# Two recurrent attention layers on one core: softmax denominators through a ones matrix and Ln/Exp, a mask cut like the scores, projections chunk by chunk, and filler matmuls spread over all segments

## The chip, the cores and the metric

The kernel runs as one program on one core of a Trainium2 chip. The metric is the device time of one execution in microseconds (us), of which the median of three runs is given. All times of the trace come from one further execution, recorded by the hardware profiler.

## The reference

Two kinds of layer alternate, A and B, twice each, every one with a layer norm ahead of it and a residual around it. The change lies in A. A walks over 2048 tokens in 64 segments of 32. Each segment sees the 32 tokens and 8 memory rows, and the memory rows of the next segment are the first 8 rows of this one's output, so the segments depend on each other one after the other.

```python
def _A_ref(x, mem0, Wq, Wk, Wv, Wo, seg_len):     # 32 heads of 128, Dm = 512, M = 8, seg_len = 32
    mask = (idx[:, None] < M) | (idx[:, None] >= idx[None, :])
    mem = mem0
    for s in range(n_seg):                         # 64
        xs = x[:, s * seg_len:(s + 1) * seg_len, :].copy()
        h = jnp.concatenate([mem, xs], axis=1)     # 40 rows
        q = jnp.einsum('btd,dhe->bhte', h, Wq)     # k and v likewise, from Wk and Wv
        scores = jnp.einsum('bhqe,bhke->bhqk', q, k) * scale
        scores = jnp.where(mask[None, None], scores, -1000000000.0)
        p = _softmax(scores, axis=-1)
        o = jnp.einsum('bhqk,bhke->bhqe', p, v)
        o = jnp.einsum('bhte,hed->btd', o, Wo)
        mem = o[:, :M, :].copy()
        outs.append(o[:, M:, :])
    return jnp.concatenate(outs, axis=1)

x = x + _A_ref(_layernorm(x), A_mem0, A_Wq, A_Wk, A_Wv, A_Wo, A_seg_len)
x = x + _B_ref(_layernorm(x), B_w_in, B_w_sp, B_b_sp, B_w_out)   # gelu, a 2048 x 2048 mixing, two projections
# and both once more
```

## The kernel before

Four stages follow one another: A, B, A, B (`a_block` and `b_block`). In an A stage the order of the instructions on TensorE, VectorE (DVE), ScalarE (ACT) is the order of the code; SyncE and GpSimd, which issue the transfers and some small copies, are ordered by the scheduler.

**Rows of a segment.** The 40 rows of a segment are split in two. `hA` holds, transposed, the 8 memory rows and the first 24 tokens, 32 columns; it is ready only when the segment before has given its memory rows. `hBs` holds the last 8 tokens, which depend on nothing; `hB` has those of four segments together (a block `tb` of 128 tokens, 16 blocks; `j4` is the segment's number within its block).

**One segment, in the order of TensorE's work** (`segment`, from L546; the names are those of its tiles):

- `psm`: Q and K of the `hA` rows, four chunks of 512 columns, 16 matmuls of 128x32 each. Four of these matmuls (one `kt`) lie side by side in the four column groups of the array. `mm_pair` (L409) builds two chunks at once; the second of the pair uses `_mm_held` (L39 to 45), which is why half of these matmuls stand under L42. ACT copies each chunk to `rows` (L565), DVE transposes it into `QQ` or `KK` (L571).
- `psv`: V of all 40 rows, four chunks again, built in pairs; ACT copies chunks 0 and 2 to `vs`, DVE chunks 1 and 3 (L583).
- For each half of the heads: a mask matmul into `psS` over 320 columns (L587, `maskN` holds -30000), 16 small score matmuls on top of it (L591), `E` = exp on ACT (L594), four matmuls of `E` with the indicator `ind` which give the denominators of 8 heads as a column `psD` (L599), a reciprocal on DVE into `Rc`, eight matmuls that spread `Rc` over the rows again (`probs`, L608), and the product `PT` on DVE (L612). These steps stand between pieces of V.
- `psO`: 16 matmuls of `vs` with `PT` (`pv`, L621). Its columns go to `uT` of this segment (8 memory rows, L624), to `uT` of the next (24 token rows, L628) and to `oB` (8 rows, DVE, L629).
- `pw`: the output projection of `uT`, 128 matmuls of 128 columns (`wo_pass`, L493), one half behind each `psO`. The second `psO` has the same two PSUM banks as the first (pool `attO`), so it begins when all three copies of the first are done.
- `build_hA` (L535 to 539): DVE puts the memory rows from `pw` into `pre` and transposes that into the next `hA`, on which the next segment's `psm` waits.

**Fillers.** Work that belongs to other segments stands behind the second `psO` and behind `pw`, in two equal parts. `j4` = 0: `y_pass`, the projection of the last block's `oB` (`pwB`, 128 matmuls, 64 in each place). `j4` = 1 and 2: `bpass`, Q and K of the next block's `hB` (`psb`, 32 matmuls of 512 columns, 16 in each place). `j4` = 3: nothing. Beside that a block has `ln_load`, `ln_apply`, `ln_turn` (the next block's normed rows by DVE and transfers), `y_load` and `y_stats` (residual and statistics of the last block).

**PSUM.** Eight banks: four of pool `acc` (`psm`, `psv`, `psb`, `pw`, `pwB` in turn), two of `att` (`psS`, `psD`), two of `attO` (`psO`).

The lines that call the fillers:

```python
            ov1 = pv(1)
            for f in fillers:
                next(f)
            for _ in wo_pass(pw, uT_cur, 1):
                pass
            if s + 1 < NSEG:
                build_hA(s + 1, pw)
            for f in fillers:
                next(f, None)
```

## Time and profile before

| | |
|---|---|
| median of 3 runs | 2440.13 us (2438.45 to 2441.03) |
| the profiled execution's own time | 2444.6 us |
| its span, first to last instruction | 2442.7 us |
| TensorE matmul (PE) busy | 2093.6 us, 86%, 52992 instructions |
| TensorE weight load (PEld) busy | 1242.0 us, 51%, 52992 instructions |
| VectorE (DVE) busy | 1130.0 us, 46% |
| ScalarE (ACT) busy | 879.5 us, 36% |
| GpSimd (POOL) busy | 241.3 us, 10% |
| mean granted TensorE clock | 0.97 of full speed |

A matmul's own duration does not say what it costs TensorE: four matmuls of 512 columns that lie side by side in the array are each 0.39 us long and overlap. So the time of a piece of work is read from the starts of consecutive groups in the timeline, and idle time from the bracket at a row's end, which names how long the engine stood before it and what released it. "issue" there means that the engine waited for nothing that the profile shows. The two A stages take about 1900 us of the span.

### The profile page before, as it was taken

To read this page: it belongs to the slowest core of one execution; us is meant where nothing else is said; L and a number is where in the kernel's file an instruction comes from. 1 tells how busy PE (TensorE), PEld (TensorE's weight loads), DVE (VectorE), ACT (ScalarE), POOL (GpSimd) and SP (SyncE) were. 2 spreads that over 40 slices of the span, in tenths; PEclk is the share of its full clock that TensorE was granted. 3 is DMA by queue.
4 is the path that set the end of the run, shared out by engine and by line. 5 is a ranking of instruction groups with operands and counts; after the bars stand their busy time and mean duration, and the time that the engine had idled before them with its cause. 6 is when DMAs were issued, how large, how long until landed. Compare 5 with 4: busy or idle time off the path is not lost.

```text
span 2442.7 us, 114595 instructions
## 1 busy us (share of the span) xinstructions
PE 2093.6 (86%) x52992; PEld 1242.0 (51%) x52992; DVE 1130.0 (46%) x2489; ACT 879.5 (36%) x1956; POOL 241.3 (10%) x567
## 2 busy tenths in 40 slices
PE   0799999999999999872968999999999999997799
PEld 0355555555555555441754555555555555554466
DVE  2454455554555555440434555555554555553422
ACT  0343344443434344360003434444434444343700
POOL 1100000000000000001220000000000000000022
PEclk9999999999999999985989999999999999999899
DMA  9111111111111110128550111111111111102253
GB/s 361 49 31 31 31 31 32 33 31 31 31 31 31 31 32 27 65 80 249 146 171 20 32 31 31 31 31 31 31 32 32 37 31 31 29 22 82 74 125 104
DMA packets 178719, 145.98 MB, mean 60 GB/s; under 512 B 97472, under 2 KB 148288, under 8 KB 175168
## 3 DMA queue, kind: packets, MB, share of 16 engines
q1 hardware_dynamic: 152544, 83.76, 12.7%
q10 hardware_dynamic: 21728, 30.78, 3.6%
q0 software_dynamic: 3968, 24.12, 2.7%
q8 instruction: 415, 6.80, 1.2%
q14 instruction: 64, 0.52, 0.1%
HBM read 88.13 MB, written 33.70 MB: 50 GB/s over the span
## 4 chain that ended last, share of the span: by engine, by line
PE 75%; ACT 9%; DMA 6%; issue 5%; DVE 4%; POOL 1%; SPq 0%; ACTq 0%; POOLq 0%; DVEq 0%
PE psv L416 12%; PE psm L42 10%; PE psm L416 9%; PE psv L42 8%; PE pg L222 7%; PE pw L493 5%; PE psO L621 4%; PE psS L591 3%; ACT vs L583 3%; PE psD L608 3%; PE pwB L493 3%; PE psD L599 3%; DMA wspT<-in_B_w_sp_dram 2%; PE psb L416 2%; PE psS L587 2%
## 5 line engine op out<-in xcount | busy, mean ns | idle before, releaser
L416 PE MATMUL psm<-Wq_sb,hA 128*32 128x512 bf16 x4096 | 420.8, 386 | 35.1 <-DVE hA L539 31.2
L42 PE MATMUL psm<-Wk_sb,hA 128*32 128x512 bf16 x4096 | 420.1, 385 | 15.7 <-ACT rowsB L481 11.6
L416 PE MATMUL psv<-Wv_sb,hA 128*32 128x512 bf16 x2048 | 406.5, 385 | 0.0
L416 PE MATMUL psv<-Wv_sb,hBs 128*32 128x512 bf16 x2048 | 405.3, 385 | 0.0
L42 PE MATMUL psv<-Wv_sb,hA 128*32 128x512 bf16 x2048 | 400.0, 379 | 0.0
L42 PE MATMUL psv<-Wv_sb,hBs 128*32 128x512 bf16 x2048 | 398.7, 379 | 0.0
L565 ACT CAST rows<-psm 128x512 bf16<-128x512 f32 x512 | 275.0, 589 | 254.9 <-PE psm L416 253.5
L416 PEld LDWEIGHTS <-hA 128*32 128x32 bf16 x6144 | 232.3, 96 | 214.2 <-DVE hA L539 60.2
L42 PEld LDWEIGHTS <-hA 128*32 128x32 bf16 x6144 | 241.0, 97 | 164.9 <-issue 41.5
L493 PE MATMUL pw<-Wo_sb,uT 128*32 128x128 bf16 x16640 | 284.5, 219 | 33.6 <-issue 19.9
L493 PEld LDWEIGHTS <-uT 128*32 128x32 bf16 x16640 | 256.1, 97 | 83.5 <-issue 24.8
L571 DVE STREAM_TRANSPOSE QQ<-rows 128x512 bf16<-128x512 bf16 x256 | 181.3, 708 | 167.6 <-ACT rows L565 167.6
L612 DVE TENSOR_TENSOR PT<-E,psD 128x320 bf16<-128x320 bf16 x256 | 125.0, 488 | 237.0 <-PE psD L608 144.8
L222 PE MATMUL pg<-wspT,z2n 128*128 128x256 bf16 (+1 forms) x1536 | 177.0, 277 | 56.8 <-DMA wspT<-in_B_w_sp_dram 56.8
L624 ACT CAST uT<-psO 128x128 bf16<-128x128 f32 x256 | 68.0, 266 | 362.1 <-PE psO L621 362.1
L222 PEld LDWEIGHTS <-z2n 128*128 128x128 bf16 (+1 forms) x1536 | 151.4, 100 | 82.2 <-issue 64.3
L416 PE MATMUL psb<-Wq_sb,hB 128*32 128x512 bf16 x1024 | 104.1, 393 | 98.2 <-DVE hB L464 74.3
L538 DVE CAST_PREDICATED pre<-maskM,pw 128x128 bf16<-128x128 uint16 x126 | 36.7, 291 | 317.0 <-PE pw L493 317.0
L583 ACT CAST vs<-psv 128x512 bf16<-128x512 f32 x256 | 149.9, 585 | 77.0 <-PE psv L416 77.0
L583 DVE CAST vs<-psv 128x512 bf16<-128x512 f32 x256 | 176.1, 688 | 0.0
L571 DVE STREAM_TRANSPOSE KK<-rows 128x512 bf16<-128x512 bf16 x256 | 171.4, 670 | 0.3 <-ACT rows L565 0.3
L594 ACT ACTIVATE E<-psS 128x320 bf16<-128x320 f32 x256 | 111.9, 437 | 120.2 <-PE psS L591 120.2
(98 smaller groups left out, 2550.9 us busy)
## 6 DMA issues: line engine op xcount, KB each, us to landing
xs<-xd SPq DMA_DIRECT2D x48, 256.0 KB
xs<-xd ACTq DMA_DIRECT2D x48, 256.0 KB
oA_d<-o_sb SPq DMA_DIRECT2D x130, 64.0 KB
xs_y<-xd SPq DMA_DIRECT2D x32, 256.0 KB
xd<-ot_y SPq DMA_DIRECT2D x32, 256.0 KB
Wq_sb<-in_A_Wq_dram POOLq DMA_DIRECT2D x6, 1024.0 KB, 17.5
Wk_sb<-in_A_Wk_dram POOLq DMA_DIRECT2D x6, 1024.0 KB, 25.8
Wv_sb<-in_A_Wv_dram POOLq DMA_DIRECT2D x6, 1024.0 KB, 20.6
```

What stands on the lines that cost most here:

```text
L42: return te.add_instruction(mybir.InstMatmult(name=nc.get_next_instruction_name(), engine=mybir.EngineType.PE, start_tensor_calc=start, st ...
L222: nc.tensor.matmul(pg[0:fsz, :], lhsT=z2n[:, st_i, f0:f0 + fsz], rhs=wspT[:, st_i, :], start=(st_i == 0), stop=(st_i == NT - 1))
L416: nc.tensor.matmul(o, lhsT=lhs(cg), rhs=rhs2[i](kt, cg), start=st, stop=sp_, tile_position=(0, 32 * cg))
L493: nc.tensor.matmul(po[32 * cg:32 * cg + 32, 0:128], lhsT=lhs[:, h, :], rhs=wo_rhs(h, cg), start=(n == 0), stop=(n == H - 1), tile_position ...
L565: nc.scalar.copy(r[:], ps2[i][:])
L571: nc.vector.transpose(out=(QQ, KK)[i][:, half, :, 0:32], in_=rows[i][:])
L583: (nc.vector.tensor_copy if i else nc.scalar.copy)(vs[:, 4 * c:4 * c + 4, :].rearrange("p h e -> p (h e)"), ps2[i][:])
L591: nc.tensor.matmul(psS[64 * g:64 * g + 40, hl, :], lhsT=KK[:, half, 8 * g + hl, :], rhs=QQ[:, half, 8 * g + hl, :], start=False, stop=True ...
L594: nc.scalar.activation(out=E[half][:], in_=psS[:], func=ACT.Exp, scale=scale)
L599: nc.tensor.matmul(psD[half][0:80, 2 * w:2 * w + 2], lhsT=E[half][:, 2 * w:2 * w + 2, :].rearrange("p h q -> p (h q)"), rhs=ind[:, 0:2], s ...
L612: nc.vector.tensor_tensor(out=PT[half][:], in0=E[half][:], in1=psD[half][:, 128:448].rearrange("p (h q) -> p h q", q=40), op=ALU.mult)
L621: nc.tensor.matmul(psO[:, g, 40 * hl:40 * hl + 40], lhsT=vs[64 * g:64 * g + 40, 8 * half + hl, :], rhs=PT[half][64 * g:64 * g + 40, hl, :] ...
```

## The change

Numbers of lines below are those of the changed kernel where they differ.

- **Denominators.** One matmul of the block matrix `ones64` (two blocks of 64 x 64 ones) with `E` puts the sum over the keys into every row of `psD`, 320 columns. ACT takes Ln of it into `L` and exp(-L) into `R`; `PT` = `E` x `R` on DVE. The four matmuls with `ind`, the reciprocal and the eight spreading matmuls go. One instruction loads ACT's function table with exp and ln ahead of each A stage.
- **Mask.** Two matmuls, of 64 columns of weights each, in the tiling of the scores, in place of one.
- **Chunks.** Q, K and V are built chunk by chunk (`mm_chunk`), Q and K in the order 0, 2, 1, 3; ACT copies V chunks 0, 1 and 2, DVE chunk 3.
- **Fillers.** Each segment now has 32 matmuls of `pwB` behind the second `psO` (`fill_a`) and one chunk of `psb`, 16 matmuls, behind `pw` (`fill_b`). `pwB` keeps its bank through all four segments. The output loads and statistics of a block come a block later, the next block's rows are loaded earlier, and `prep_segment` stands at the segment's end.

```diff
+        def mm_chunk(ps, lhs, rhs, kts=range(KT)):
+            for kt in kts:
                 for cg in range(4):
...
+                    nc.tensor.matmul(ps[32 * cg:32 * cg + 32, :], lhsT=lhs(kt, cg), rhs=rhs(kt, cg),
+                                     start=(kt == 0), stop=(kt == KT - 1), tile_position=(0, 32 * cg))
...
+        nc.scalar.add_instruction(mybir.InstLoadActFuncSet(name=nc.get_next_instruction_name(), engine=mybir.EngineType.Activation,
+                                                           act_func_set_id=LN_EXP_SET, ins=[], outs=[]))
...
         def bpass(tb, j):
...
+            ps = acc.tile([P, 512], F32, name="psb")
+            mm_chunk(ps, lambda kt, cg: bs["hB"][:, kt, :], lambda kt, cg: qk_rhs(j, kt, cg))
+            r = rowp.tile([P, 512], BF16, name="rowsB", bufs=2)
+            nc.scalar.copy(r[:], ps[:])
...
         def y_pass(tb):
             pwB = acc.tile([P, DM], F32, name="pwB")
-            for n, _ in enumerate(wo_pass(pwB, blk_state[tb]["oB"])):
-                if n == 1:
-                    yield
+            for _ in wo_pass(pwB, blk_state[tb]["oB"]):
+                yield
...
-                (nc.vector.tensor_copy if i else nc.scalar.copy)(vs[:, 4 * c:4 * c + 4, :].rearrange("p h e -> p (h e)"), ps2[i][:])
+                (nc.vector.tensor_copy if c == 3 else nc.scalar.copy)(vs[:, 4 * c:4 * c + 4, :].rearrange("p h e -> p (h e)"), ps[:])
...
-                nc.tensor.matmul(psS[:], lhsT=ident_bf[:], rhs=maskN[:].unsqueeze(1).to_broadcast([P, 8, 40]),
-                                 start=True, stop=True, skip_group_check=True)
+                for g in range(2):
+                    nc.tensor.matmul(psS[64 * g:64 * g + 64], lhsT=ident_bf[:, 64 * g:64 * g + 64],
+                                     rhs=maskN[:].unsqueeze(1).to_broadcast([P, 8, 40]),
+                                     start=True, stop=True, tile_position=(0, 64 * g), skip_group_check=True)
...
             def denom(half):
-                psD[half] = att.tile([P, 512], F32, name="psD")
-                for w in range(4):
-                    nc.tensor.matmul(psD[half][0:80, 2 * w:2 * w + 2], lhsT=E[half][:, 2 * w:2 * w + 2, :].rearrange("p h q -> p (h q)"),
-                                     rhs=ind[:, 0:2], start=True, stop=True)
...
+                psD = att.tile([P, 8, 40], F32, name="psD")
+                nc.tensor.matmul(psD[:], lhsT=ones64[:], rhs=E[half][:], start=True, stop=True)
+                L = segp.tile([P, 8, 40], F32, name="L")
+                nc.scalar.activation(out=L[:], in_=psD[:], func=ACT.Ln)
+                R[half] = segp.tile([P, 8, 40], BF16, name="R")
+                nc.scalar.activation(out=R[half][:], in_=L[:], func=ACT.Exp, scale=-1.0)
...
             def probs(half):
-                for w in range(4):
-                    for g in range(2):
-                        nc.tensor.matmul(psD[half][64 * g:64 * g + 64, 128 + 80 * w:208 + 80 * w],
-                                         lhsT=Rc[half][0:80, 2 * w + g:2 * w + g + 1].to_broadcast([80, 64]), rhs=ident_bf[0:80, 0:80],
-                                         start=True, stop=True, tile_position=(0, 64 * g))
                 PT[half] = segp.tile([P, 8, 40], BF16, name="PT")
-                nc.vector.tensor_tensor(out=PT[half][:], in0=E[half][:], in1=psD[half][:, 128:448].rearrange("p (h q) -> p h q", q=40), op=ALU.mult)
+                nc.vector.tensor_tensor(out=PT[half][:], in0=E[half][:], in1=R[half][:], op=ALU.mult)
...
             scores(0)
-            v_kt(0, v0, 2)
-            v_kt(0, v0, 3)
-            v_out(0, v0, 0)
+            qk_T(3, r3)
+            v_mm(0, range(2, 4), v0)
             denom(0)
+            v_out(0, v0)
+            v1 = v_mm(1, range(0, 2))
             scores(1)
...
+            def fill_a():
+                next(yp, None)
+
+            def fill_b():
+                if tb + 1 < NB:
+                    bpass(tb + 1, (0, 2, 1, 3)[j4])
+                if j4 == 3:
+                    next(yp, None)
...
-        y_load(NB - 1)
-        y_stats(NB - 1)
+        for tb in (NB - 2, NB - 1):
+            y_load(tb)
+            y_stats(tb)
```

What stands in a row on the engines afterwards, at three places:

ACT, one segment before, from the last copies of Q and K to the copies of the second `psO` (`E` is the exp, `vs` the copies of V, `uT` those of `psO`):

```order
L565 CAST rows<-psm 128x512 x4
L594 ACTIVATE E<-psS 128x320
L583 CAST vs<-psv 128x512
L594 ACTIVATE E<-psS 128x320
L624 CAST uT_316<-psO 128x2x8x8
L583 CAST vs<-psv 128x512
L628 CAST uT_315<-psO 128x2x8x24
L624 CAST uT_316<-psO 128x2x8x8
L543 COPY o_sb<-pw 128x128
L628 CAST uT_315<-psO 128x2x8x24
```

and the same stretch of the changed kernel:

```order
L538 CAST rows<-psm 128x512 x4
L565 ACTIVATE E<-psS 128x320
L571 ACTIVATE L<-psD 128x320
L573 ACTIVATE R<-L 128x320
L552 CAST vs<-psv 128x512
L565 ACTIVATE E<-psS 128x320
L571 ACTIVATE L<-psD 128x320
L573 ACTIVATE R<-L 128x320
L552 CAST vs<-psv 128x512 x2
L589 CAST uT_308<-psO 128x2x8x8
L593 CAST uT_307<-psO 128x2x8x24
L589 CAST uT_308<-psO 128x2x8x8
```

Each exp has two more passes behind it, the first copy of V stands behind those of half 0 and ahead of the exp of half 1, and both other copies of V stand ahead of the first copy of `psO`.

TensorE around the first denominators, before (each matmul has its weight load ahead of it; `ident_bf` and `maskN` are the mask's):

```order
L42 LDWEIGHTS hBs_301
L42 MATMUL psv<-Wv_sb,hBs_301 32x512
L599 LDWEIGHTS E
L599 MATMUL psD<-ind,E 80x2
L599 LDWEIGHTS E
L599 MATMUL psD<-ind,E 80x2
L599 LDWEIGHTS E
L599 MATMUL psD<-ind,E 80x2
L599 LDWEIGHTS E
L599 MATMUL psD<-ind,E 80x2
L587 LDWEIGHTS ident_bf
L587 MATMUL psS<-maskN,ident_bf 128x320
```

and now:

```order
L399 LDWEIGHTS hBs_293
L399 MATMUL psv<-Wv_sb,hBs_293 32x512
L569 LDWEIGHTS ones_83
L569 MATMUL psD<-E,ones_83 128x320
L399 LDWEIGHTS hA_291
L399 MATMUL psv<-Wv_sb,hA_291 32x512
```

One matmul stands for four, and a piece of V stands between it and the second mask.

TensorE at the end of a segment that had no filler (`j4` = 3), the last matmul of `pw` and the next segment's first `psm`, before:

```order
L493 LDWEIGHTS uT_32285
L493 MATMUL pw<-Wo_sb,uT_32285 32x128
L416 LDWEIGHTS hA_32270
L416 MATMUL psm<-Wq_sb,hA_32270 32x512
```

and now, with the row of `psb` standing for 16 of its kind:

```order
L471 LDWEIGHTS uT_31254
L471 MATMUL pw<-Wo_sb,uT_31254 32x128
L399 LDWEIGHTS hB
L399 MATMUL psb<-Wq_sb,hB 32x512
...
L399 LDWEIGHTS hA_31239
L399 MATMUL psm<-Wq_sb,hA_31239 32x512
```

A chunk of `psb` stands between the two in every segment.

## Rows read from the trace of the kernel before

**Rows 1.** The page: one transfer queue, and the chain by engine.

```profile
q8 instruction: 415, 6.80, 1.2%
...
PE 75%; ACT 9%; DMA 6%; issue 5%; DVE 4%; POOL 1%; SPq 0%; ACTq 0%; POOLq 0%; DVEq 0%
```

**Rows 2.** Waits of TensorE by releaser: us in total, times, longest.

```profile
PE psO L621 <- DVE oB L629: 48.8, 128, 0.5
...
PE pwB L493 <- issue: 29.5, 19, 4.0
...
PE pw L493 <- issue: 19.9, 23, 3.9
```

**Rows 3.** Timeline, TensorE, two segments' starts: start, length, instruction [idle before, releaser].

```profile
82.56 0.61 PE L416 MATMUL psm<-Wq_sb,hA 128*32 128x512 bf16 x4 [2.21 <-DVE hA L539]
...
1017.97 0.62 PE L416 MATMUL psm<-Wq_sb,hA 128*32 128x512 bf16 x4 [0.74 <-DVE hA L539]
```

**Rows 4.** Timeline, TensorE, one segment of the first attention stage, the middle.

```profile
502.54 0.31 PE L587 MATMUL psS<-maskN,ident_bf 128*128 128x320 bf16 x1
502.78 0.38 PE L591 MATMUL psS<-QQ,KK 128*40 128x40 bf16 x16
503.09 0.39 PE L416 MATMUL psv<-Wv_sb,hA 128*32 128x512 bf16 x1
...
504.07 0.31 PE L599 MATMUL psD<-ind,E 128*80 128x2 bf16 x4
...
504.77 0.39 PE L416 MATMUL psv<-Wv_sb,hA 128*32 128x512 bf16 x1
...
505.32 0.33 PE L608 MATMUL psD<-ident_bf,Rc 80*64 80x80 bf16 x8
505.58 0.39 PE L416 MATMUL psv<-Wv_sb,hA 128*32 128x512 bf16 x1
```

**Rows 5.** Timeline, the same segment: ACT, DVE and the second psO.

```profile
503.26 0.44 ACT L594 ACTIVATE E<-psS 128x320 bf16<-128x320 f32 x1 [0.55 <-PE psS L591]
...
507.93 0.59 ACT L583 CAST vs<-psv 128x512 bf16<-128x512 f32 x1 [0.34 <-PE psv L416]
...
508.15 0.69 DVE L583 CAST vs<-psv 128x512 bf16<-128x512 f32 x1
...
508.42 0.48 ACT L628 CAST uT<-psO 128x384 bf16<-128x384 f32 x1
...
508.93 0.29 DVE L629 CAST oB<-psO 128x128 bf16<-128x128 f32 x1
...
509.37 0.37 PE L621 MATMUL psO<-PT,vs 40*128 40x40 bf16 x16 [0.38 <-DVE oB L629]
...
509.67 1.08 PE L493 MATMUL pwB<-Wo_sb,oB 128*32 128x128 bf16 x64
```

**Rows 6.** Timeline, TensorE, the end of a segment without filler.

```profile
437.28 1.08 PE L493 MATMUL pw<-Wo_sb,uT 128*32 128x128 bf16 x64 [0.35 <-ACT uT L624]
439.11 0.40 PE L416 MATMUL psm<-Wq_sb,hA 128*32 128x512 bf16 x4 [0.75 <-DVE hA L539]
```

**Rows 7.** Timeline, TensorE, two places with issue ahead of a row.

```profile
155.16 0.79 PE L493 MATMUL pw<-Wo_sb,uT 128*32 128x128 bf16 x42 [0.70 <-issue]
...
569.94 0.62 PE L493 MATMUL pwB<-Wo_sb,oB 128*32 128x128 bf16 x30 [0.26 <-issue]
570.35 1.11 PE L493 MATMUL pw<-Wo_sb,uT 128*32 128x128 bf16 x64
571.24 0.67 PE L493 MATMUL pwB<-Wo_sb,oB 128*32 128x128 bf16 x34
...
573.96 0.92 PE L493 MATMUL pwB<-Wo_sb,oB 128*32 128x128 bf16 x30 [2.05 <-issue]
```

**Rows 8.** Timeline, the first attention stage's last transfers: ACT and DVE.

```profile
1042.76 0.27 ACT L504 COPY oB_sb<-pwB 128x128 f32<-128x128 f32 x1 [6.90 <-PE pwB L493]
...
1048.95 0.69 DVE L112 BATCH_NORM_STATS2 bnst<-ot_y 128x6 f32<-128x512 f32 x1 [15.28 <-POOL ot_y L517]
```

More of the change, by code (lines that the diff above doesn't have):

```diff
@@ L544, in store_o, with segment @@
             nc.sync.dma_start(oA_d[s], o_sb[:])
-        def segment(s, fillers):
+        def segment(s, fill_a, fill_b):
             tb, j4 = s // 4, s % 4
@@ L554, in segment @@
             oB = blk_state[tb]["oB"]
-            E, PT, psD, Rc = [None] * 2, [None] * 2, [None] * 2, [None] * 2
-            def qk(half):
-                ps2 = [acc.tile([P, 512], F32, name="psm") for _ in range(2)]
-                for kt in range(KT):
-                    mm_pair(ps2, lambda cg: hA_cur[:, kt, :],
-                            [lambda kt, cg, jj=jj: qk_rhs(jj, kt, cg) for jj in (half, half + 2)], kt)
-                rows = []
-                for i in range(2):
-                    r = rowp.tile([P, 512], BF16, name="rows", tag="rowsQK", bufs=4)
-                    nc.scalar.copy(r[:], ps2[i][:])
-                    rows.append(r)
-                return rows
@@ L569, in qk_T @@
-            def qk_T(half, rows):
-                for i in range(2):
-                    nc.vector.transpose(out=(QQ, KK)[i][:, half, :, 0:32], in_=rows[i][:])
-            def v_start():
-                return [acc.tile([P, 512], F32, name="psv") for _ in range(2)]
-            def v_kt(half, ps2, kt):
-                def rhs(c):
-                    return lambda kt, cg: Wv_sb[:, kt, 2048 * (cg // 2) + 512 * c:2048 * (cg // 2) + 512 * c + 512]
-                mm_pair(ps2, lambda cg: (hA_cur if cg % 2 == 0 else hB_cur)[:, kt, :], [rhs(2 * half), rhs(2 * half + 1)], kt)
@@ L581, in v_out, with qk @@
-            def v_out(half, ps2, i):
-                c = 2 * half + i
-                (nc.vector.tensor_copy if i else nc.scalar.copy)(vs[:, 4 * c:4 * c + 4, :].rearrange("p h e -> p (h e)"), ps2[i][:])
+            E, PT, R = [None] * 2, [None] * 2, [None] * 2
+            def qk(j):
+                ps = acc.tile([P, 512], F32, name="psm")
+                mm_chunk(ps, lambda kt, cg: hA_cur[:, kt, :], lambda kt, cg: qk_rhs(j, kt, cg))
+                r = rowp.tile([P, 512], BF16, name="rows", tag="rowsQK", bufs=4)
+                nc.scalar.copy(r[:], ps[:])
+                return r
@@ new lines, in qk_T, with v_mm, v_out @@
+            def qk_T(j, r):
+                nc.vector.transpose(out=(QQ, KK)[j // 2][:, j % 2, :, 0:32], in_=r[:])
+            def v_mm(c, kts, ps=None):
+                if ps is None:
+                    ps = acc.tile([P, 512], F32, name="psv")
+                mm_chunk(ps, lambda kt, cg: (hA_cur if cg % 2 == 0 else hB_cur)[:, kt, :],
+                         lambda kt, cg: Wv_sb[:, kt, 2048 * (cg // 2) + 512 * c:2048 * (cg // 2) + 512 * c + 512], kts)
+                return ps
+            def v_out(c, ps):
+                (nc.vector.tensor_copy if c == 3 else nc.scalar.copy)(vs[:, 4 * c:4 * c + 4, :].rearrange("p h e -> p (h e)"), ps[:])
@@ L585, in scores @@
             def scores(half):
                 psS = att.tile([P, 8, 40], F32, name="psS")
[L587 to L588 removed]
+                for g in range(2):
+                    nc.tensor.matmul(psS[64 * g:64 * g + 64], lhsT=ident_bf[:, 64 * g:64 * g + 64],
+                                     rhs=maskN[:].unsqueeze(1).to_broadcast([P, 8, 40]),
+                                     start=True, stop=True, tile_position=(0, 64 * g), skip_group_check=True)
@@ L662, in segment @@
             ov1 = pv(1)
-            for f in fillers:
-                next(f)
+            fill_a()
             for _ in wo_pass(pw, uT_cur, 1):
```

123 lines of the change are left out of this document (40 added, 83 removed).

## The prediction
> **What bounds the kernel now.** I read the chain of waits first: 75% of the span is TensorE's own work [rows 1]. Then the first matmul (`psm`) of the first and of the last of the 64 segments of the first attention stage: 82.56 and 1017.97 us [rows 3], 63 periods in 935.41 us, so 14.85 us a segment. There are 128 segments, about 1900 of the 2443 us, and the change touches nothing that is long outside them. So the question is what a period is made of: TensorE's work plus the times it stands still.
>
> The work comes from the timeline of one segment [rows 4]. Between 504.77 and 505.32 stand eight matmuls of 512 columns and the change to another tiling of the array: 0.55 us. Between 503.09 and 504.07 stand sixteen and one change: 0.98. The difference says 0.43 us for eight, and 0.11 to 0.12 for a change. Per segment on average there are 64 such matmuls for Q and K, 64 for V and 16 for the next block's `psb`: 144, so 7.78 us. Five changes out of V: 0.55. The mask takes 0.24 (502.54 to 502.78), the scores 0.31 (to 503.09), each with the change behind it. The first denominator, second mask and second scores together take 0.70 (504.07 to 504.77), which leaves 0.15 to the denominator; the second denominator stands alone between V pieces and I take 0.24 for it. The two `probs` broadcasts take 0.26 each (505.32 to 505.58). `psO` takes 0.30 (509.37 to 509.67) [rows 5], twice. 64 small matmuls of `pw` or `pwB` take 0.89 (570.35 to 571.24) [rows 7]: 1.80 for `pw`, 0.45 for the average quarter of `pwB`. Sum: 7.78 + 0.55 + 0.55 + 0.70 + 0.24 + 0.52 + 0.60 + 1.80 + 0.45 = **13.19 us of work, so 1.66 of waiting** in 14.85.
>
> Three waits make most of that. The second `psO` waits for the copy into `oB` (48.8 us in 128 times) [rows 2]. `hA` arrives 1.83 us after the second half of `pw` began (437.28 to 439.11) [rows 6], where `pw` itself is done after 0.9; only segments with a filler there hide it. And "issue" is TensorE without instructions: 29.5 and 19.9 us in `pwB` and `pw` alone [rows 2].
>
> **How the issue wait works.** The instruction queue moved 6.80 MB in 415 packets [rows 1], 16 KB each. What a packet holds shows in rows 7: between two stalls stand 30 + 64 + 34 = 128 matmuls from 569.94 on, with their weight loads 256 instructions, and then nothing until 573.96. Undisturbed they would have taken 1.8 us; the next block was there 4.0 us after this one began. Counting 128 matmuls back from each of the 42 stalls in `pw` and `pwB` [rows 2], I find the next block 2.9 to 4.1 us after the start of its predecessor, mostly 3.5 (but for three at the ends of the stages). So a block that TensorE gets through in less than about 3.5 us may end in a stall. I sorted the blocks of the two stages by the time that they took without their stall: all eighteen up to 2.25 us stalled, by 1.65 on average; of thirteen at 2.43 to 2.48, ten, by 0.20 to 1.44 (155.16 is one of them [rows 7]), 0.51 on average over the thirteen; of 41 between 2.75 and 3.25, ten.
>
> **The change, part by part.**
> *Fewer instructions on TensorE.* Per half the four denominator matmuls become one over 320 columns; I price it like the mask, which has the same columns and the same kind of change behind it: 0.24 [rows 4]. The eight broadcasts go: 2 x 0.26. The mask in the scores' tiling needs two matmuls, but they lie in different columns of the array and no change follows: between 0.14 (0.24 less a change) and 0.24; I take 0.14, since the four matmuls of a 512-column group run side by side too, and keep 0.24 for the range. V is cut differently, but the number of changes out of V stays five: two masks, two denominators, one `psO`. New work: 7.78 + 0.55 + 2 x (0.14 + 0.31) + 2 x 0.24 + 0.60 + 1.80 + 0.45 = **12.56, so 0.63 less**.
>
> *Two more passes on ACT per half.* They stand between E and the copies of V in one queue, so I place them in time, with t = 0 at the first `psm`. QK ends at 3.46, V piece to 4.00, mask and scores(0) to 4.45, with the scores beginning at 4.14. E starts 0.48 after the scores begin (502.78 to 503.26) and takes 0.44 [rows 4, 5]: ready at 5.06. TensorE has finished the next V piece at 4.99, so the denominator waits 0.12 to 5.11. Ln has its input at 5.49; Ln and exp at E's 0.44 each end at 6.42; the copy of V (0.59, and 0.10 of it overlapped by the next instruction: 507.93 and 508.42 [rows 5]) ends at 6.92. E(1) has its scores at 6.51 but stands behind that copy: 6.83 to 7.27. TensorE is through at 6.88 and waits 0.44. Behind it V piece 2 and the first half of piece 3 run to 8.97, by when the first half's probabilities (exp at 6.42, then one multiply on DVE) are long there: the later start of `psO` hides that chain. The copy of V piece 1 ends at 9.13 and costs `psO` 0.08, the memory columns of `uT` cost `pw` 0.07. If ACT's passes were 0.1 slower, these waits would grow by about 0.3; if the copy came out early enough they would shrink by 0.4.
>
> *Second `psO`.* It still waits for V piece 3, then DVE's copy (0.69 from 508.15), then `oB` (508.93), and starts 0.44 after that (509.37) [rows 5]. The same ladder from the end of V piece 3 at 9.79 gives 11.20, where TensorE is ready at 10.75: 0.45 remains, 0.05 to 0.1 less than before.
>
> *Fillers.* 32 `pwB` matmuls (0.45) now stand behind the second `psO` in every segment. `psO` and they take 0.75, about what the copy of `uT` needs. One chunk of `psb` (0.87) stands behind `pw`, where `hA` comes 0.94 after `pw`'s end: 0.07 remains. Before, some segments had too much there and others nothing. The chunk's copy on ACT frees the PSUM bank of the second QK chunk: ready about 0.80 after the filler, needed at 0.87, so it is covered with little to spare. `pwB` keeps one of the four banks for a whole block; with three left, each chunk finds the bank of two chunks earlier, copied by then.
>
> *Waits so far:* 0.12 + 0.44 + 0.08 + 0.07 + 0.45 + 0.07 = 1.23. Period without instruction stalls: 13.79.
>
> *Instruction stalls.* The fillers close the very gaps in which the queue caught up. Every segment now runs `pw`, the wait of 0.45, `psO`, `pwB`, `pw`, `psb`: 384 instructions in some 3.9 us. A block that ends anywhere from inside `pwB` to inside `psb` runs 2.3 to 2.9 us, which is the kind that stalled by 0.51 on average. A segment has 748 instructions, no multiple of 256, so block ends drift through all places; some 200 of 256 places lie in that zone. With the 3.5 us rule I get stalls of 0.4 to 1.2 over it, 0.66 averaged over all places; with the measured mean, 0.40. I take **0.55 per segment**; before, `pw` and `pwB` alone had 49 us over 128 segments, 0.39 [rows 2].
>
> *The rest.* Both blocks' output loads now stand behind the last segment. The first of them can run under the last 256 small matmuls; without that cover it costs one chain, 1042.76 to 1048.95, 6.2 us [rows 8], per stage; I take 1 each. The earlier load of block 1 and the order of the four first `psb` chunks hide behind the wait for the first rows. SyncE and GpSimd get the same transfers and copies; theirs are due a whole segment later.
>
> **Sum.** 13.79 + 0.55 = 14.34, 0.51 less than 14.85, times 128 is 65; less 2 for the ends: 63. The profiled execution took 2444.6 us (span 2442.7), 4.5 over the median of 2440.13; 2444.6 - 63 - 4.5 = **2377**.
>
> **Rivals.**
> *Instructions keep up.* For it: three of the thirteen blocks did not stall, and 31 of the 41 slower ones didn't. Against it: all eighteen of the shortest did. Then 13.79 stands: 1.06 x 128 = 136, or 2306. The Trainium skill (Runtime: NRT & Kernel Launch, Instruction fetch mechanics) says that a block boundary costs little, mostly hidden, because the sequencer fetches the next block while it runs this one; by that rule the time would be 2306. The 573.96 row, with 2.05 us of waiting at a boundary, speaks against it here. Chance 0.17 for 2300 to 2345.
> *ACT becomes the bound.* ACT carries E, Ln, exp and three V copies in one queue between scores and `psO`. If the two waits grow by 0.4 together, the period is 14.74 and the time 2428. For it: 0.44 of waiting already comes from this order. Against it: ACT is idle through most of the second half of the segment. Chance 0.13 for 2415 to 2445.
> *Slower: a full refill stall in every segment.* Place: the dense run from `pw` to `psb`. Price: a block that starts with `pw` is through after 2.3 us and would wait 1.2 to 1.3 in each segment, if block ends met it every time: 15.1, or 2472. It decides from 1.06 us of stall per segment on. Against it: the drift of 748 against 256. Chance 0.07.
> *It does not do what it says:* ACT's order of instructions shows one table load at the start of each stage and none between exp and Ln, so I give no chance to reloads.
>
> **How the numbers follow.** Forecast, 2345 to 2415: 0.60. Instructions keep up: 0.17. ACT: 0.13. Slower: 0.07. The remaining 0.03 lies under 2300 or between. About 0.2% (5 us) is what a measurement can tell from no change. Faster: all of the first two and two thirds of ACT's case: 0.86; same 0.06; slower 0.08. The range 2310 to 2430 leaves out half of the slow cases and some of the fastest. Its ends: low by 0.05 of stall, high by a mask at 0.24 and stalls of 0.75.
>
> **What would show it.** The period in the changed kernel near 14.3 us with a spread, not constant; `psD` with a wait on E of about 0.1 and 0.4; the second `psO` with the wait on `oB` unchanged near 0.4; no wait of `psm` on `hA` above 0.1; "issue" at 60 to 80 us in `pw`, `pwB`, `psb` and `psm` together, spread over all segments. If issue stays under 20 us, the first rival holds; over 130, the last. If `psD` waits over 0.8 per segment, ACT's.

## The result and the profile after

The changed kernel takes **2342.18 us** (median of four runs, 2339.76 to 2348.28), the kernel before 2440.58 beside it (four runs, 2438.45 to 2450.66): a ratio of 0.9593, with a 95% interval of 0.956 to 0.9625. Forecast were 2377, with a range of 2310 to 2430. The sign and the range held, and so did the mechanism, but for the terms named below; the gain is 98 us where I had 63.

The waits of TensorE in the changed kernel (us in total, times, longest), against [rows 2]; the line of the second `psO` with 48.8 us is gone:

```profile
PE pw L471 <- issue: 57.9, 55, 3.8
PE psD L569 <- ACT E L565: 38.1, 128, 0.3
PE psb L399 <- issue: 34.1, 17, 23.6
...
PE psm L399 <- DVE hA L516: 7.7, 8, 1.6
...
PE pwB L471 <- issue: 4.0, 2, 2.5
PE pw L471 <- ACT uT L589: 3.5, 10, 0.4
...
PE psm L399 <- issue: 1.6, 4, 0.8
```

23.6 us of the `psb` line are one wait at the start of the second attention stage. What is left of "issue" is 74 us, where the kernel before has 57 counted the same way; 64 of the 74 lie in the segments' periods, 10 at the two stages' ends. The new wait on `E` is that of the second denominator. `uT` holds TensorE up only in the first four segments of a stage and at its end, and `hA` only at its start and in its last segments, where one of the fillers is missing.

Now the period, as in [rows 3]: the first `psm` of the first and of the last segment of the first stage, start first.

```profile
81.50 0.83 PE L399 MATMUL psm<-Wq_sb,hA 128*32 128x512 bf16 x12 [1.63 <-DVE hA L516]
...
967.08 0.61 PE L399 MATMUL psm<-Wq_sb,hA 128*32 128x512 bf16 x8 [0.74 <-DVE hA L516]
```

885.58 us for 63 periods: **14.06**, against 14.85 before and 14.34 forecast. But no segment is like the next. The shortest take 13.35, many 14.0 to 15.0. TensorE's rows in one of the shortest (timeline; the `psv` rows are left out):

```profile
222.14 1.05 PE L399 MATMUL psm<-Wq_sb,hA 128*32 128x512 bf16 x16
...
226.15 0.33 PE L557 MATMUL psS<-maskN,ident_bf 128*64 128x320 bf16 x2
226.31 0.36 PE L562 MATMUL psS<-QQ,KK 128*40 128x40 bf16 x16
...
227.20 0.30 PE L569 MATMUL psD<-E,ones 128*128 128x320 bf16 x1
...
227.97 0.33 PE L557 MATMUL psS<-maskN,ident_bf 128*64 128x320 bf16 x2
228.13 0.36 PE L562 MATMUL psS<-QQ,KK 128*40 128x40 bf16 x16
...
229.33 0.30 PE L569 MATMUL psD<-E,ones 128*128 128x320 bf16 x1 [0.30 <-ACT E L565]
...
230.97 0.43 PE L586 MATMUL psO<-PT,vs 40*128 40x40 bf16 x16
...
231.79 1.08 PE L471 MATMUL pw<-Wo_sb,uT 128*32 128x128 bf16 x64
232.95 0.37 PE L586 MATMUL psO<-PT,vs 40*128 40x40 bf16 x16
233.25 0.63 PE L471 MATMUL pwB<-Wo_sb,oB 128*32 128x128 bf16 x32
233.70 1.07 PE L471 MATMUL pw<-Wo_sb,uT 128*32 128x128 bf16 x64
234.60 1.04 PE L399 MATMUL psb<-Wq_sb,hB 128*32 128x512 bf16 x16
235.51 0.83 PE L399 MATMUL psm<-Wq_sb,hA 128*32 128x512 bf16 x12
```

From 222.14 to 235.51: 13.37, with no "issue" in it. From `pw` at 231.79 to 235.51 stand 192 matmuls, with their weight loads 384 instructions, in 3.72 us; the other 182 take 9.65. Below, the first is called the dense stretch and the rest the sparse one. And the end of another one, from 500.31 to 514.57 (14.26), with a wait in the second half of `pw`:

```profile
511.40 0.63 PE L471 MATMUL pwB<-Wo_sb,oB 128*32 128x128 bf16 x32
...
511.86 0.45 PE L471 MATMUL pw<-Wo_sb,uT 128*32 128x128 bf16 x20
...
513.02 0.80 PE L471 MATMUL pw<-Wo_sb,uT 128*32 128x128 bf16 x44 [0.71 <-issue]
513.65 1.04 PE L399 MATMUL psb<-Wq_sb,hB 128*32 128x512 bf16 x16
```

The bracket says 0.71, yet this period is 0.89 longer than the one shown ahead. The bracket counts from the modelled end of the matmul before, which is 0.22 long, while these matmuls start 0.014 apart; the time from 511.86 to 513.02 holds 20 of them, which take 0.28. That makes 0.88 of waiting. So **a wait in these rows costs about 0.2 more than its bracket shows**.

Over the 126 periods of both stages 102 us are gained. A few of these come from TensorE's granted clock: inside the periods it falls from full speed (2.4 GHz) to half (1.2 GHz) for a short stretch five times before and twice after, for instance behind the wait of 2.05 us at 573.96 [rows 7] before and behind one of 1.58 us at 1931.91 after. The work behind the latter takes 1.6 us longer than in the segment shown above, so three stretches fewer are worth some 5 us (an estimate from this one). Outside the periods 6 us are lost: the span fell by 96.2. The loss shows at the stages' ends. The last copy of `pwB` and the last statistics in the changed kernel, against [rows 8]:

```profile
992.00 0.27 ACT L481 COPY oB_sb<-pwB 128x128 f32<-128x128 f32 x1 [4.85 <-PE pwB L471]
...
995.24 0.69 DVE L98 BATCH_NORM_STATS2 bnst<-ot_y 128x6 f32<-128x512 f32 x1 [14.04 <-POOL ot_y L494]
...
1002.98 0.69 DVE L98 BATCH_NORM_STATS2 bnst<-ot_y 128x6 f32<-128x512 f32 x1 [6.83 <-POOL ot_y L494]
```

11.0 us where it was 6.2: the two output loads come one after the other.

### The profile page after: what moved, and what is told of

Its sections match the earlier page's. It is cut to its first block, busy times and chain, and to the rows that moved or that the text cites. A ratio compares the mean times of both kernels' runs of the same rounds, so it can differ in the third digit from the quotient of the medians.

```text
span 2346.5 us, 108555 instructions
## 1 busy us (share of the span) xinstructions
PE 2018.0 (86%) x50432; PEld 1146.9 (49%) x50432; DVE 942.5 (40%) x2035; ACT 1167.1 (50%) x2660; POOL 249.8 (11%) x567
## 3 DMA queue, kind: packets, MB, share of 16 engines
q1 hardware_dynamic: 152544, 83.76, 13.1%
## 5 line engine op out<-in xcount | busy, mean ns | idle before, releaser
L399 PEld LDWEIGHTS <-hA 128*32 128x32 bf16 x12288 | 378.4, 96 | 423.3 <-issue 100.7
L399 PE MATMUL psv<-Wv_sb,hA 128*32 128x512 bf16 x4096 | 580.9, 382 | 0.0
L399 PE MATMUL psv<-Wv_sb,hBs 128*32 128x512 bf16 x4096 | 580.7, 382 | 0.0
L471 PE MATMUL pw<-Wo_sb,uT 128*32 128x128 bf16 x16640 | 292.4, 221 | 61.3 <-issue 57.9
L399 PE MATMUL psm<-Wq_sb,hA 128*32 128x512 bf16 x4096 | 276.7, 382 | 9.4 <-DVE hA L516 7.7
L399 PE MATMUL psm<-Wk_sb,hA 128*32 128x512 bf16 x4096 | 272.3, 380 | 0.0
L461 ACT CAST rowsB<-psb 128x512 bf16<-128x512 f32 x128 | 75.0, 586 | 353.7 <-PE psb L399 353.7
L577 DVE TENSOR_TENSOR PT<-E,R 128x320 bf16<-128x320 bf16 x256 | 83.3, 325 | 403.1 <-ACT R L573 403.1
L208 PE MATMUL pg<-wspT,z2n 128*128 128x256 bf16 (+1 forms) x1536 | 175.1, 275 | 57.9 <-DMA wspT<-in_B_w_sp_dram 57.9
L571 ACT ACTIVATE L<-psD 128x320 f32<-128x320 f32 x256 | 112.0, 437 | 98.1 <-PE psD L569 98.1
L399 PEld LDWEIGHTS <-hBs 128*32 128x32 bf16 x4096 | 156.0, 95 | 1.8
L552 DVE CAST vs<-psv 128x512 bf16<-128x512 f32 x128 | 88.6, 692 | 132.9 <-PE psv L399 132.9
```

What stands on the lines that cost most here:

```text
L208: nc.tensor.matmul(pg[0:fsz, :], lhsT=z2n[:, st_i, f0:f0 + fsz], rhs=wspT[:, st_i, :], start=(st_i == 0), stop=(st_i == NT - 1))
L399: nc.tensor.matmul(ps[32 * cg:32 * cg + 32, :], lhsT=lhs(kt, cg), rhs=rhs(kt, cg), start=(kt == 0), stop=(kt == KT - 1), tile_position=(0, ...
L461: nc.scalar.copy(r[:], ps[:])
L471: nc.tensor.matmul(po[32 * cg:32 * cg + 32, 0:128], lhsT=lhs[:, h, :], rhs=wo_rhs(h, cg), start=(n == 0), stop=(n == H - 1), tile_position ...
L552: (nc.vector.tensor_copy if c == 3 else nc.scalar.copy)(vs[:, 4 * c:4 * c + 4, :].rearrange("p h e -> p (h e)"), ps[:])
L571: nc.scalar.activation(out=L[:], in_=psD[:], func=ACT.Ln)
```

## The experiments

Two theories stood against each other. **Refill:** TensorE's instructions come in blocks of 256, at fixed places of the program, and a block that runs faster than the next one arrives ends in a wait. **Contention:** the waits come when other transfers are in the way, wherever a block ends. First a count in the two traces. TensorE's instructions are numbered in the order of the program, semaphore waits that are instructions of their own included. In 52 of the 53 "issue" waits over 0.15 us of the kernel before, and in 77 of the 78 of the changed one, the number of the matmul behind the wait leaves 194 or 195 when divided by 256; the one other in each is the long wait at the start of the second stage. One semaphore wait that is an instruction of its own stands in each segment, so a segment has 749 instructions, not the 748 of my text.

The traces also show the blocks arrive. A transfer queue of its own, q8 [rows 1], moves one packet of 16 KB per block, 394 in the changed kernel, and when a block begins, the packet of the next one has not landed yet in 383 cases. For the 73 blocks that end in a wait inside the stages, that packet starts 0.85 us after the block's first matmul (median; 0.26 to 1.79), takes 1.0, and the first matmul of the next block starts 1.4 after its end, 3.3 in all. So the next block is fetched while the one before runs, and no further ahead.

All kernels below are the changed one with one edit each, unless said otherwise. "Shortest" and "mean" are the segments' periods of both stages, from one profile each; two profiles of kernels with the same segments (the changed one and `ends`) differ by 0.05 in the mean. The changed kernel's profile is that of the longest of its four runs (2348.28). The kernel before stood beside each: 2434.42 to 2437.07 here, 2440.58 beside the changed kernel. So a difference to 2342.18 holds some 4 to 6 us that are not the edit's; the ratios are free of that.

| kernel | us | ratio to before (95%) | shortest | mean |
|---|---|---|---|---|
| changed | 2342.18 | 0.9593 (0.956 to 0.9625) | 13.35 | 14.06 |
| lock_good | 2271.24 | 0.9328 (0.9305 to 0.9351) | 13.35 | 13.44 |
| lock_bad | 2391.36 | 0.9817 (0.9781 to 0.9853) | 13.36 | 14.41 |
| v3_act | 2334.66 | 0.9587 (0.9564 to 0.961) | 13.20 | 13.93 |
| v0_late | 2312.27 | 0.9488 (0.946 to 0.9516) | 13.04 | 13.82 |
| old_fill | 2384.66 | 0.9787 (0.9744 to 0.9829) | four kinds | 14.39 |
| old_denom | 2374.81 | 0.9735 (0.9686 to 0.9784) | 13.60 | 14.26 |
| one_mask | 2351.35 | 0.9653 (0.9615 to 0.9691) | 13.44 | 14.13 |
| sparse | 2296.77 | 0.9422 (0.9384 to 0.946) | 13.34 | 13.66 |
| ends | 2340.45 | 0.9594 (0.9559 to 0.9629) | 13.35 | 14.01 |
| two_waits | 2307.70 | 0.9484 (0.9422 to 0.9545) | 12.89 | 13.73 |
| best | 2209.94 | 0.9057 (0.9014 to 0.91) | 12.89 | 12.99 |
| chunks_only | 2451.46 | 1.0063 (1.004 to 1.0086) | four kinds | 14.90 |

### Where the blocks end: lock_good and lock_bad

```diff
+                    pieces = 1 if n < 0 else 16 if n < fine else 2 if n < fine + cut else 1
+                    for q in range(pieces):
...
+                         cut=(9, 10)[s % 2] if j == 3 else 0)
```

The cuts split some Q and K matmuls in two and make a segment 768 instructions long on average, three blocks. Cuts in the four `psb` chunks ahead of each stage shift the whole: `PHASE_PAIRS = [7, 120]` in one, `[93, 120]` in the other. The work is the same.

> The changed kernel with 9 or 10 of the Q/K matmuls of each segment cut in two, so that a segment has 768 instructions on TensorE, three times 256, and cuts ahead of each attention stage that set where the blocks end: the same three places in every segment, the dense one in the middle of pwB. The computation is the same. Refill theory (a block of 256 instructions that runs in under about 3.35 us ends in a wait for the next one): by the changed kernel's trace the three blocks take 3.4, 3.4 and 6.6 us, so the wait falls from 0.70 per segment to 0.0 to 0.35, the period from 14.06 to 13.4 to 13.7, nearly the same in all segments, and the time to 2270 to 2305. Rival (the waits come from other transfers in the way, wherever the block ends): the period stays at 14.0 to 14.1 with its spread, the time at 2340 to 2350.

> As lock_good, the same number of instructions per segment, but the blocks end at the first matmul of pw. Refill theory: the block from pw to the middle of the second half of pw runs in 2.1 us and waits 1.2 in every segment, the period is 14.5 to 14.7 in all segments, the time 2390 to 2420. Rival: as for lock_good, 14.0 to 14.1 and 2340 to 2350.

The waits of TensorE on "issue" in `pw`, first of lock_good, then of lock_bad:

```profile
PE pw L479 <- issue: 8.5, 2, 4.4
```

```profile
PE pw L479 <- issue: 107.9, 122, 2.0
```

The first and the last segment of the first stage, lock_good:

```profile
80.54 0.83 PE L407 MATMUL psm<-Wq_sb,hA 128*32 128x512 bf16 x12 [1.63 <-DVE hA L524]
...
927.00 0.83 PE L407 MATMUL psm<-Wq_sb,hA 128*32 128x512 bf16 x12 [0.74 <-DVE hA L524]
```

846.46 us for 63 periods, 13.44. **120 us lie between two kernels that do the same work with the same number of instructions in a segment**; only the place where the blocks end differs. In lock_good the two blocks that begin or end in the dense stretch run 3.29 us and more in nearly all segments, and a single bracket of 0.17 us is left inside the stages: the two waits of its line in `pw` stand behind the last segments. Some waiting is left without a bracket: in 42 of 122 segments the first matmul behind a block's end in `psm` starts 0.06 to 0.43 us after the one before, where 0.003 is usual, because the matmuls before it are modelled as 0.38 us long; 8 us together. In lock_bad the block from `pw` on runs 2.3 us, and 122 times TensorE waits in `pw` (0.88 in the rows; 0.97 per segment by the means of the two kernels). That is less than the 1.2 that I expected, and the period of 14.41 is just under my range.

Refill holds: where a block ends decides whether TensorE waits. Contention alone expected the same time for both. But it is not without effect. Of the 120 blocks of lock_bad that end in a wait inside the stages, 64 have no transfer beside the instructions' own from their start to the wait's end, and wait 0.66 us on average in the rows (0.29 to 1.15); the other 56 wait 1.10 (up to 2.02). One of the 64, and the longest:

```profile
175.06 0.85 PE L479 MATMUL pw<-Wo_sb,uT 128*32 128x128 bf16 x47 [0.36 <-issue]
...
1509.01 0.85 PE L479 MATMUL pw<-Wo_sb,uT 128*32 128x128 bf16 x48 [2.02 <-issue]
```

In the second one 177 packets of another queue moved while the block ran and TensorE waited. So the waits come without other transfers, and are longer where there are some; that the transfers are the reason was not tested.

The Trainium skill (Runtime: NRT & Kernel Launch, Instruction fetch mechanics) says that crossing a boundary of 256 instructions is mostly hidden, because the sequencer fetches ahead. lock_good agrees with that and lock_bad does not (8 us of hidden waiting in the one, 122 waits in the other): it depends on how long the block before the boundary runs.

### Two waits, one in the sparse stretch and one in the dense

```diff
             denom(0)
-            v_out(0, v0)
             v1 = v_mm(1, range(0, 2))
             scores(1)
+            v_out(0, v0)
```

> The changed kernel with ACT's copy of V chunk 0 behind the exp of the second half instead of ahead of it. The second denominator's wait on E (0.37 with the drain) falls by about 0.2: shortest period 13.15. This wait lies in the sparse stretch (V), where no block ends early, so by the refill theory too the whole gain stays: 20 to 27 us (2315 to 2322). Rival (ACT's queue only moves the wait to the first psO or to L of the second half): the mean stays within 0.05, 2336 to 2348.

The line of `psD` on `E`, 38.1 us in the changed kernel, is gone from the waits. The shortest period fell by 0.31, the mean by 0.24, the time by 30 us (26 by the ratios). That is more than I expected (0.2, and 2315 to 2322). Whether the whole 0.31 came through the means don't tell: this profile has five stretches at half clock where the changed kernel's has two, some 0.04 of the mean. ACT's order had put the copy of V chunk 0 ahead of an exp that TensorE waits for, and nothing needed that copy so early.

```diff
-            v_out(3, v3)
             tok_out(0, ov0)
+            v_out(3, v3)
...
-                (nc.vector.tensor_copy if c == 3 else nc.scalar.copy)(vs[...], ps[:])
+                nc.scalar.copy(vs[...], ps[:])
```

> The changed kernel with the copy of V chunk 3 on ACT, behind the copy of psO's token columns, so that DVE is free for oB. The shortest period falls from 13.35 by the 0.26 that TensorE waits for the second psO, to 13.1. If waits simply add up, the mean falls as much, 32 us in all (2310). Refill theory: the wait lies inside the dense stretch, where a block that runs faster waits longer at its end, and about half of the segments have such an end: the mean falls by 0.10 to 0.16, 13 to 20 us in all (2322 to 2330).

The place in question (timeline of v3_act):

```profile
494.33 0.50 ACT L593 CAST uT<-psO 128x384 bf16<-128x384 f32 x1
494.51 1.08 PE L471 MATMUL pw<-Wo_sb,uT 128*32 128x128 bf16 x64
494.73 0.60 ACT L552 CAST vs<-psv 128x512 bf16<-128x512 f32 x1
494.87 0.29 DVE L594 CAST oB<-psO 128x128 bf16<-128x128 f32 x1 [1.18 <-ACT uT L593]
495.52 0.37 PE L586 MATMUL psO<-PT,vs 40*128 40x40 bf16 x16
```

DVE is free, yet `oB` starts when ACT's copy of the same `psO` ends, at 494.83: it waits for that copy too. `psO` now starts 1.01 after `pw`, where `pw` takes 0.89; 0.12 is the change of tiling. So only 0.15 of the 0.26 was a wait, and my expectation of 13.1 was off by the rest. How much of the 0.15 came through is not settled: the means differ by 0.13, of two profiles that can be 0.05 off, the medians by 7.5 us, and the ratios (0.9587 and 0.9593) hardly at all. The run doesn't tell the theories apart.

> The changed kernel with both v0_late and v3_act, the instructions' blocks as they fall. Shortest period 13.35 - 0.31 - 0.15 = 12.89. If waits add up, the mean falls by the same 0.46 (58 us, 2284). Refill theory: v3_act's part lies in the dense stretch, where a third to a half is given back: mean 13.65 to 13.72, 2290 to 2300.

12.89 as computed. But the mean is 13.73 and the time 2307.70, both just above my range: of 0.46 that the two waits had, 0.33 came through by the profiles, and "issue" in `pw` alone rose from 57.9 to 72.0 us. That fits a gain that is partly waited for again at a block's end.

### The fillers, and TensorE's own work

```diff
+            def fill(i):
+                if j4 == 0:
+                    next(yp, None)
+                elif j4 < 3 and tb + 1 < NB:
+                    bpass(tb + 1, (0, 2, 1, 3)[2 * (j4 - 1) + i])
```

> The changed kernel with the fillers of before: 64 and 64 matmuls of pwB in the first segment of a block, two psb chunks in the second and third each, none in the fourth. From the changed kernel's rows: work without fillers 11.23 us, waits without the two gaps 0.76; shortest periods 13.85, 13.8, 13.8 and 13.4 (both gaps, 0.45 and 0.94, open) for the four kinds, mean 13.7 against 13.35. If the even spread is worth what the gaps say, the time is 2365 to 2390. Rival: the even spread only makes the dense stretch the same everywhere and the instruction waits take its gain; then the time is within 8 us of 2342.

42 us slower (47 by the ratios). Two lines of its waits show the gaps that are open again:

```profile
PE psm L399 <- DVE hA L517: 38.8, 75, 1.6
...
PE pw L471 <- ACT uT L590: 16.1, 38, 2.3
```

> The changed kernel with the 32 pwB matmuls moved from behind the second psO to the place ahead of the second denominator, where TensorE waits 0.37 for E. If only waits and work count, that wait is filled and a wait of 0.45 for uT opens behind psO: the period rises by 0.08, the time to 2350. Refill theory: the dense stretch has 320 instructions instead of 384 and a gap in it, so the instruction waits fall from 0.70 to 0.2 to 0.5 per segment, which gives 2290 to 2325.

```diff
             v_mm(1, range(2, 4), v1)
+            fill_a()
             denom(1)
...
             ov1 = pv(1)
-            fill_a()
```

45 us faster (42 by the ratios), although a new wait opens:

```profile
PE pw L471 <- ACT uT L589: 47.7, 128, 1.7
...
PE pw L471 <- issue: 13.7, 18, 2.2
```

The wait for `uT` is what the change had closed. It costs 47.7 us, the wait on `E` falls from 38.1 to 2.4, and "issue" in `pw` falls from 57.9 to 13.7. **A filler is worth less in a gap inside the dense stretch than in a gap of the sparse one**: there the next block's instructions were on their way in the gap. The time, 2297, lies in the range of the refill theory; the mean period is 13.66.

> The changed kernel with the denominators of before (four matmuls with ind, the reciprocal on DVE, eight spreading matmuls per half), all else as changed. Work: two times 0.26 for the spreading matmuls more; the second denominator's wait on E shrinks by up to 0.3, since ACT has two passes fewer. Shortest period 13.5 to 13.9, time 2355 to 2400. Rival (ACT's two added passes cost as much as TensorE saves): within 8 us of 2342 or faster.

The edit puts back the lines that the diff of the change removes there, and the spreading of the first half stands ahead of the second denominators again. 33 us slower (35 by the ratios): TensorE's 0.52 of spreading matmuls come back, the second denominator's wait is gone from its waits; 0.25 remains in the shortest period.

> The changed kernel with the mask as one matmul over the whole array, as before. My sum took 0.14 for the two tiled ones against 0.24: 0.1 per half, 26 us in all if both are on the path (2368). By the changed kernel's timeline the second half's mask is followed by a wait of 0.3 for E, which ACT's copy of V ahead of it sets, so that only the first half's counts: 0.1 per segment, 13 us (2355). Rival, no difference: within 5 us of 2342.

```diff
-                for g in range(2):
-                    nc.tensor.matmul(psS[64 * g:64 * g + 64], lhsT=ident_bf[:, 64 * g:64 * g + 64], ...
+                nc.tensor.matmul(psS[:], lhsT=ident_bf[:], rhs=maskN[:].unsqueeze(1).to_broadcast([P, 8, 40]),
```

9 us slower by the medians and 15 by the ratios, 0.09 in the shortest period, and the wait on `E` shrinks from 38.1 us to this:

```profile
PE psD L567 <- ACT E L563: 25.2, 128, 0.2
```

0.1 per segment is taken out of that wait: the second half's mask lies under it, and only the first half's counts.

> The changed kernel with the denominators, the mask and the fillers of before together, so that of the change the chunk-by-chunk order, the fourth V copy's engine and the moved loads are left. Undone one by one the three cost 33, 9 and 42 us, 84 of the 98. If they add up: 2426, so that the chunks are worth 14 us against before. If they overlap (fewer instructions and shorter waits help each other), it is away from that: 2437 or more if the chunks alone are worth nothing.

15 us slower than before. The three parts undone one by one cost 84 us, together 109; by the ratios 97 and 115. Taken as they stand, undoing all three costs more than the sum, so each is worth more when the others are gone. But a single ratio is known to about 0.002 to 0.005 either way, 6 to 12 us, so that the parts simply add up is not ruled out. Why the rest of the change alone is slower than the kernel before was not separated further.

### The ends, and the parts together

```diff
-            xs = xp.tile([P, DM], F32, name="xs_y", bufs=1)
+            xs = xp.tile([P, DM], F32, name="xs_y", bufs=2)
...
-            ot = xp.tile([P, 4, P], F32, name="ot_y", bufs=1)
+            ot = xp.tile([P, 4, P], F32, name="ot_y", bufs=2)
```

> The changed kernel with two buffers instead of one for the rows and the residual of the output loads. My sum took 1 us per attention stage for the second output chain; by the traces the time from the last copy of pwB to the last statistics is 6.2 us before and 11.0 us after, since the chains follow one another through one buffer. With two buffers they overlap: 6.2 to 8 us, the time 6 to 10 us lower (2332 to 2336). Rival (the chain is bound by SyncE's and GpSimd's order, not by the buffer): within 3 us of 2342.

The times do not tell it from the changed kernel, as the rival had it. The trace shows an effect, but a smaller one than I expected:

```profile
990.78 0.27 ACT L481 COPY oB_sb<-pwB 128x128 f32<-128x128 f32 x1 [6.55 <-PE pwB L471]
...
993.55 1.26 POOL L494 TENSOR_TENSOR ot_y<-ot_y,xs_y 128x512 f32<-128x512 f32 x1 [60.71 <-DMA ot_y<-oB_d]
...
999.51 0.69 DVE L98 BATCH_NORM_STATS2 bnst<-ot_y 128x6 f32<-128x512 f32 x1 [3.75 <-POOL ot_y L494]
```

8.7 us instead of 11.0. The first load's sum still starts only at 993.55. Its `oB` rows go out from 988.71 on, when the store of that block's `oB_sb`, issued at 979.41, has landed. That store stands behind the next stage's weights (`w_in_sb`, 1376 KB, issued at 978.91): from 979.40 to 988.70 the transfer engines are 79% busy, and the first packets of the store's size move from 985 on. This was read from the trace and not tried.

> two_waits and ends together with the cuts of lock_good: 768 instructions per segment, block ends in the middle of pwB. The two blocks with an end in the dense stretch take 3.27 and 3.21 us by the traces, a little under the 3.29 that did not stall in lock_good. Period 12.9 to 13.05, time 2198 to 2220. If blocks under 3.29 already stall by some tenths each, 13.1 to 13.3, 2225 to 2250.

The first stage of best, first and last segment:

```profile
83.72 0.61 PE L407 MATMUL psm<-Wq_sb,hA 128*32 128x512 bf16 x8 [1.63 <-DVE hA L524]
...
902.00 0.61 PE L407 MATMUL psm<-Wq_sb,hA 128*32 128x512 bf16 x8 [0.74 <-DVE hA L524]
```

12.99 per segment and **2209.94 us, a ratio of 0.9057 to before**. With the blocks held in place the two waits are worth their full 0.46 (13.44 to 12.99 in the mean), where with drifting blocks they were worth 0.33 by the profiles.

## Why the prediction was right, and what in it was off

**Work.** 12.56 forecast. The shortest segment's rows give 3.46 for Q and K, 0.45 for mask and scores of a half, 0.22 for each denominator, 0.30 for `psO`, 0.89 for half a `pw`, 0.46 for `pwB`; with V at 0.54 for eight matmuls and a change, the sum is 12.54. Each term was right to a few hundredths, the tiled mask among them: 0.16, for which I took 0.14 and had 0.24 as the far end.

**Waits.** 1.23 forecast, 0.82 measured. This is the first mis-sized term, and the larger one:

| wait | forecast | measured |
|---|---|---|
| first denominator on `E` | 0.12 | 0.06 |
| second denominator | 0.44 | 0.37 |
| first `psO` | 0.08 | 0.06 |
| `pw` on `uT` | 0.07 | 0 |
| second `psO` | 0.45 | 0.27, of which 0.12 is the change of tiling |
| `psm` on `hA` | 0.07 | 0.06 |

The step that failed is the one on the second `psO`. I took the time from DVE's copy of V to `oB` and on to `psO` from [rows 5], 0.78 and 0.44. There `oB` had two things to wait for, DVE's copy (until 508.84) and ACT's copy of `uT` (508.42 and 0.48, until 508.90); the later one was ACT's. In the changed kernel ACT has copied earlier (ACT and DVE in the short segment shown above):

```profile
231.61 0.50 ACT L593 CAST uT<-psO 128x384 bf16<-128x384 f32 x1
...
232.00 0.69 DVE L552 CAST vs<-psv 128x512 bf16<-128x512 f32 x1 [1.04 <-PE psv L399]
232.61 0.28 DVE L594 CAST oB<-psO 128x128 bf16<-128x128 f32 x1
```

ACT is done at 232.11, `oB` follows DVE's copy with an overlap of 0.08, and `psO` starts at 232.95, 0.34 after `oB` began. I had treated a chain with two arms as one with one. That accounts for 0.17 of the chain (0.78 became 0.61); why `psO` follows `oB` 0.10 sooner (0.34, not 0.44) is not shown. The other differences are small ones of a ladder in which each rung stands on the last: counted from the first `psm`, `E` of the first half was ready at 5.01 (forecast 5.06), its Ln began at 5.39 (5.49), and `E` of the second half was ready at 7.14 (7.27).

**Instruction stalls.** 0.55 forecast, 0.62 measured: the mean lies 0.71 above the shortest period, but lock_good, with almost no bracketed wait, has 0.09 of that too. "Issue" was forecast at 60 to 80 us over all segments; the rows say 74, of which 64 lie in the 126 periods, 0.51 in each. That this and the 0.62 can both be is the second mis-sized term: I calibrated with the rows' 0.51 per short block, and the rows leave out 0.2 of each wait. With 73 waits that is 0.11 per period. The mechanism was right in its parts: all 46 blocks of the changed kernel that ran up to 2.36 us undisturbed waited, by 1.0 on average in the rows; of the 30 between 2.5 and 2.7, 14. The count of 748 instructions was off by one; block ends drift through the segment with either number.

**Ends.** 1 us per stage forecast, 4.8 measured (11.0 against 6.2). I let the first output load run under the last 256 matmuls. It didn't: by the trace the load of its `oB` rows went out only at 989.52, in the last wait of these matmuls, because the store of those rows, issued at 980.99, stood behind the next stage's weights; and the second load had to wait for the first one's buffer. Over everything outside the periods 6 us were lost and not twice 4.8, so some 4 came back elsewhere, which was not traced.

**The sum again.** 0.41 less waiting, 0.02 less work, 0.07 more of stall and 0.09 of spread that stands in lock_good too: 14.34 becomes 14.07, and 14.06 it was. That is 35 us more gain over 128 segments, less 4 for the ends, 31 of the 35 us between 2377 and 2342; the rest is within what the runs differ by. The number came out near partly by luck: waits too high by 0.41 and stalls too low by 0.16 stood against each other.

**The rivals.** The time lies in the band of "instructions keep up", 2300 to 2345, and yet that case didn't occur: "issue" grew. What it would have looked like is lock_good, at 2271, lower than my 2306 mostly by the waits that I had too high. ACT did not become the bound, but its order was worth 0.31 per segment, as v0_late shows; the prediction had named that size ("if the copy came out early enough they would shrink by 0.4"). A stall in every segment, the slower rival, is lock_bad: 14.41, not the 15.1 that I priced, since I started from 13.79 without stalls where lock_good has 13.44, and since the wait came to 0.97 and not 1.2 to 1.3. It stayed faster than before. ACT's tables were not reloaded inside the segments.

## What to carry to other kernels

Before work is spent on closing gaps of an engine, count its instructions per microsecond around the gap: where 256 of them run in less than the time that the next 256 need to come, the gap was not idle, and closing it gives back part of what it gains. Spread the instructions first (put fillers of many small matmuls into the sparse stretch), and in a loop make their number a multiple of 256, with the ends of the blocks where the two neighbours run longest; that alone was worth 71 us here (65 by the ratios), beside the 98 of the whole change. A wait read from a trace of before has as many arms as the instruction waits for, other readers of the same tile included: the one that ended last there need not be the one that ends last afterwards.

## What of the hardware was not expected

That the places are exact: but for one at the start of the second stage, all bracketed waits on "issue" fall on one place modulo 256, the same in the kernel before and after. That no more than one block is fetched ahead: in 383 of the changed kernel's 394 blocks the next packet had not landed when a block began. That so little lies between waiting every time and hardly at all: blocks of 2.3 us in lock_bad waited every time, blocks of 3.29 us in lock_good not at all or by at most 0.43. In between there is no sharp edge: in the changed kernel 14 of 30 blocks of 2.5 to 2.7 us waited, and 2 of 10 at 3.25 to 3.4. For the time to the next block is not a constant: from a block's start to the first instruction after its wait 2.6 to 4.0 us passed by the rows of the changed kernel, mostly 3.0 to 3.7.
